# Four pieces of x in a row, early value weights and beta on another queue, keys ahead of queries: the start of a two-block attention kernel

## The chip, the cores and the metric

The kernel runs on one core of a Trainium2 chip. The metric is device time in microseconds (us) of one launch, as a median of several runs. The trace is one profiled execution, and all its times are counted from the start of its span. Engines are named TensorE (PE in the profile; PEld is its weight load), VectorE (DVE), ScalarE (ACT), GpSimd (POOL) and SyncE (SP, which only issues DMAs here).

## The reference, cut to what matters

Two attention blocks on separate inputs; the outputs are laid side by side. S is 2048, D is 1024, 32 heads of 32.

```
A:  q, k, v = x @ wqkv                       # heads of 32
    p = softmax(q k^T / sqrt(32));  out = (p v) @ wo
B:  q, k, v = x @ wq, x @ wk, x @ wv;  4 segments of 512 rows
    per segment: a_dot = softmax(q k^T / sqrt(32) + causal mask) v
                 a_mem = phi(q) M / (phi(q) z + 1e-6);  phi(t) = t + 1 if t > 0 else exp(t)
                 o = g a_mem + (1 - g) a_dot,  g = sigmoid(beta) per head
                 M += phi(k)^T v;  z += sum phi(k)
    out = o @ wo
```

## The kernel before, in words

Heads are handled four at a time (a group, 128 columns of the projections), eight groups in each block. Block A's scores are made in tiles of 128 keys x 256 queries per head. TensorE writes scores to PSUM (L1197), ScalarE turns two banks at a time into exponentials P (L1260 for the first eight, which take a bias; L1273 for the others), TensorE multiplies P with the values (L1364) and with ones for the row sums (L1371), VectorE and GpSimd normalize. For some A tiles a polynomial on VectorE and GpSimd (L1234, L1237) replaces one exponential. Projections (L825) run as jobs between the scores.

No maximum is taken per row. Instead a guard bounds the scores: squares of keys and queries (L1598 on GpSimd, L1836 on VectorE) are summed over a head's rows by a matmul (L1611), reduced to a column (L1618), made spreadable (`spreadable`, L1628: a copy to 32 columns times UP), spread over the partitions by another matmul (L1687) and reduced again (L1695). From that come a raw bias (L1701), a bias (L1704) and a flag (L1711). If the bound is small enough the exponential runs without a bias. ScalarE reads each guard's flag ahead of the first exponential that it covers and branches on it (`run_split`), so a late flag holds ScalarE. The first guard of A (of its first quarter of the rows) gives its raw bias directly to the first eight exponentials, without a branch. Later quarters of group 0 go through `guard_more`, which first takes the maximum with the running column (L1660).

The order of the work is not written out by hand. Every operation has a key (a place in the order of ScalarE's exponentials), a modelled duration and dependencies; `Prog.schedule` runs a list scheduler over all engines and so fixes one instruction order for each engine, which then executes in order. `deps` are waited for on the chip; `order` only says that an operation is not put ahead of another's start. `plan_jobs` adds the projections with release and due times. The table SHIFT moves keys of single items by hand-set amounts, one entry per item and engine.

The start (`plan_prologue`): `loads` issues group 0's key and query weights W_A on ScalarE's queue and six transposing loads of x on SyncE's (X_PIECES: quarter of the rows, range of the 128-column blocks, modelled issue and landing): pieces 0 and 1 are the first 512 rows, 2 and 3 the second 512, pieces 4 and 5 the third and the fourth whole. The first half of the value weights (Wv_A) is issued on SyncE between pieces 1 and 2. Piece 4 waits for piece 3 to land. TensorE runs idle warming products until piece 0 is there. `quarter(key, c, banks)` makes keys and queries of quarter c, in the order: keys, queries of blocks 0 to 3, then keys, queries of blocks 4 to 7. `job_V0` makes values: for each of four row blocks k eight products (L1881); its argument `behind` orders them behind another operation. `beta` (L1819 to L1828) loads beta and works out g; its item has key 60, so it runs during A's second group.

Of the kernel before, what the change touches and what calls it, by code (L numbers as in the profile page):

```python
# [7 lines left out]
ACT = mybir.ActivationFunctionType  # L8
# [3 lines left out]
P = 128  # L12
# [33 lines left out]
X_PIECES = ((0, 0, 4, 2.27, 5.3), (0, 4, 8, 4.81, 2.2), (1, 0, 4, 4.8, 2.1), (1, 4, 8, 1.82, 3.3), (2, 0, 8, 5.0, 3.0),  # L46
# [82 lines left out]
class Op:  # L129
# [4 lines left out]
    def __init__(self, eng, fn, dur, lat, key, mode=None, sem=None):  # L134
# [44 lines left out]
        1: -0.5}),  # L179
    ("plan_constants", "POOL", {  # L180
        0: -1.25, 3: 1.5, 4: -4.75, 5: -5.5, 6: 10, 8: -0.5, 9: -2.25, 10: -1.25, 15: 4, 16: -0.75, 17: 3.25, 19: 15.25,
        20: -3, 21: 12.25, 22: 1.5, 23: 5}),
    ("plan_exp", "POOL", {
# [8 lines left out]
    ("plan_jobs", "ACT", {  # L192
# [3 lines left out]
    ("plan_jobs", "DVE", {  # L196
# [65 lines left out]
    ("plan_prologue", "ACT", {  # L262
        4: 6, 5: 9.5, 8: -1.25, 10: -1.75}),
    ("plan_prologue", "DVE", {
        0: 2.5, 1: -5.5, 5: -0.25, 6: 0.25, 7: -0.25, 8: 4, 9: -0.5, 10: 1}),
    ("plan_prologue", "PE", {
# [2029 lines left out]
```

## Time and profile before

| | us |
|---|---|
| median of 3 runs (1050.74 to 1052.89) | 1052.52 |
| profiled execution | 1052.34 |
| its span | 1050.6 |
| ScalarE busy | 1016.4 |
| TensorE busy | 1020.6 |
| first products on x start | 7.36 |
| first exponential starts | 14.92 |
| ninth exponential starts | 24.88 |
| last exponential ends | 1041.9 |

A row of a timeline has its start, its length, engine, source line, operation, output<-input, shapes and count; in brackets stands the idle time of the engine before it and what ended it. Rows of one kind that follow one another are merged. A row of the DMA view ends with the us from issue to landing. A row of the table by stretches has the stretch, its length, each engine's busy time with its count of instructions, the granted clock, the share of the DMA engines and GB/s. TensorE's granted clock is 1.00 throughout.

### The profile page before, as it was taken

The numbers are of one execution on the slowest core, as the hardware profiler recorded it, in microseconds if no ns is written. First come the engines' busy times: TensorE is split into PE (matmuls) and PEld (weight loads), VectorE is DVE, ScalarE is ACT, GpSimd is POOL, SyncE is SP. The second block draws the span as 40 slices with busy tenths as digits, with TensorE's granted clock in tenths as the row PEclk, the third lists the DMA queues.
The fourth block names the chain that finished last, engine by engine and source line by source line (L and its number), as shares of the span: only waits on it lengthen the run. The fifth ranks groups of instructions, "written<-read, shape, count | busy, mean of one in ns | idle before, by whom it ended". The sixth has DMA issues, their size and how long they took to land.

```text
span 1050.6 us, 56208 instructions
## 1 busy us (share of the span) xinstructions
PE 1020.6 (97%) x25482; PEld 561.9 (53%) x25482; DVE 701.0 (67%) x1560; ACT 1016.4 (97%) x1225; POOL 585.7 (56%) x677
## 2 busy tenths in 40 slices
PE   8999999999999999999999999999999999999998
PEld 4555555655555545565555555565555545445554
DVE  2356767667566686787865598686765785874444
ACT  4999989999999999999999999999999999999997
POOL 2115577568554675766646487665644775663310
PEclk9999999999999999999999999999999999999999
DMA  9232442005313331033223320132113561021101
GB/s 184 40 91 59 78 119 45 20 6 126 89 43 90 66 100 29 11 83 66 63 62 95 96 62 19 27 92 54 51 28 86 162 177 30 24 78 61 51 23 63
DMA packets 171390, 72.17 MB, mean 69 GB/s; under 512 B 134800, under 2 KB 169360, under 8 KB 171152
## 3 DMA queue, kind: packets, MB, share of 16 engines
q1 hardware_dynamic: 168784, 67.79, 26.5%
q8 instruction: 200, 3.28, 1.3%
q10 hardware_dynamic: 2368, 0.79, 0.3%
q14 instruction: 38, 0.31, 0.1%
HBM read 45.29 MB, written 11.73 MB: 54 GB/s over the span
## 4 chain that ended last, share of the span: by engine, by line
PE 66%; ACT 30%; DVE 3%; issue 1%; ACTq 0%; DVEq 0%
PE ps L825 32%; ACT P L1273 28%; PE ps L1197 13%; PE ps L1364 9%; PE ps L1371 9%; PE ps L1881 1%; ACT P L1260 1%; ACT PKQ_B L1925 1%; DVE Y L1234 1%; DVE T L1434 1%; PE ps L1641 0%; DVE OT_B L1952 0%; DVE KQ_B L1584 0%; DVE T L1430 0%; DVE T L1436 0%
## 5 line engine op out<-in xcount | busy, mean ns | idle before, releaser
L1273 ACT ACTIVATE P<-ps 128x1024 bf16<-128x1024 f32 (+1 forms) x1176 | 988.6, 1062 | 13.7 <-DVE cu L1390 4.1
L1237 POOL TENSOR_TENSOR Pc<-Y 128x512 bf16<-128x512 f32 x238 | 249.5, 1049 | 259.9 <-PE ps L825 72.6
L1371 PE MATMUL ps<-P,onesb 128*32 128x256 bf16 (+1 forms) x4388 | 295.2, 270 | 0.2
L1364 PE MATMUL ps<-P,V_A 128*32 128x256 bf16 x3620 | 252.0, 274 | 0.3 <-ACT P L1273 0.2
L1234 DVE TENSOR_SCALAR Y<-ps 128x512 f32<-128x512 f32 x238 | 163.3, 686 | 104.7 <-PE ps L1197 97.8
L1197 PE MATMUL ps<-KQ_A 32*128 32x256 bf16 x4096 | 203.6, 273 | 12.5 <-ACT P L1273 7.2
L1197 PEld LDWEIGHTS ps<-KQ_A 32*128 32x128 bf16 x4096 | 61.9, 92 | 157.8 <-ACT P L1273 113.5
L1371 PEld LDWEIGHTS ps<-P,onesb 128*32 128x32 bf16 x4388 | 129.0, 96 | 26.3 <-issue 13.1
L825 PE MATMUL ps<-xT_B,W_B 128*32 128x512 bf16 (+1 forms) x2284 | 139.8, 359 | 1.2 <-DVE KQ_B L1584 0.4
L825 PE MATMUL ps<-xT_A,W_A 128*32 128x512 bf16 (+1 forms) x2256 | 138.3, 361 | 0.3 <-DVE V_A L1584 0.2
L1364 PEld LDWEIGHTS ps<-P,V_A 128*32 128x32 bf16 x3620 | 107.7, 96 | 26.0 <-issue 10.8
L1364 PE MATMUL ps<-Pc,V_A 128*32 128x256 bf16 x476 | 119.1, 274 | 1.1 <-issue 1.0
L1371 PE MATMUL ps<-Pc,onesb 128*32 128x256 bf16 x476 | 119.1, 274 | 0.7 <-issue 0.7
L1296 POOL TENSOR_SCALAR_AFFINE_SELECT P<-P 128x768 bf16<-128x768 bf16 (+1 forms) x96 | 75.7, 794 | 49.7 <-ACT P L1273 47.7
L1598 POOL TENSOR_TENSOR sqA<-KQ_A 128x512 bf16<-128x512 bf16 x61 | 63.3, 1047 | 62.7 <-DVE KQ_A L1584 29.3
L1598 POOL TENSOR_TENSOR sqB<-KQ_B 128x512 bf16<-128x512 bf16 x64 | 67.8, 1060 | 19.6 <-DVE KQ_B L1584 15.4
L825 PEld LDWEIGHTS ps<-xT_B,W_B 128*32 128x32 bf16 x2284 | 52.9, 96 | 47.1 <-issue 18.9
L825 PEld LDWEIGHTS ps<-xT_A,W_A 128*32 128x32 bf16 x2256 | 52.5, 96 | 46.5 <-issue 16.4
L1447 DVE STREAM_TRANSPOSE T<-rc 128x256 f32<-128x256 f32 (+1 forms) x152 | 72.6, 481 | 2.7
L825 PE MATMUL ps<-Wv_B,xT_B 128*32 128x512 bf16 (+1 forms) x1128 | 70.1, 361 | 1.1 <-issue 0.5
L825 PE MATMUL ps<-Wo_B,OT_B 128*32 128x512 bf16 (+1 forms) x1128 | 69.0, 361 | 0.2 <-DVE T L1430 0.2
L1584 DVE CAST KQ_B<-ps 128x512 bf16<-128x512 f32 x64 | 43.8, 684 | 35.0 <-PE ps L825 34.4
(117 smaller groups left out, 1229.2 us busy)
## 6 DMA issues: line engine op xcount, KB each, us to landing
Wv_B<-in_B_wv_dram SPq DMA_DIRECT2D x32, 256.0 KB, 3.4
W_B<-in_B_wk_dram SPq DMA_DIRECT2D x32, 256.0 KB, 3.3
W_B<-in_B_wq_dram SPq DMA_DIRECT2D x32, 256.0 KB, 4.0
Wo_B<-in_B_wo_dram SPq DMA_DIRECT2D x32, 256.0 KB, 3.1
out_dram<-outsb SPq DMA_DIRECT2D x56, 128.0 KB, 1.8
W_A<-in_A_wqkv_dram SPq DMA_DIRECT2D x14, 256.0 KB, 3.3
ot_a_scratch<-OTst SPq DMA_DIRECT2D x51, 64.0 KB, 1.8
xT_A<-ot_a_scratch SPq DMA_DIRECT2D x6, 512.0 KB, 5.4
```

Of the source, the lines that this page charges most:

```text
L825: ins = e.matmul(out[r], w[:, r], x, start=start, stop=stop, tile_position=(0, 32 * t), skip_group_check=True)
L1197: ins = e.matmul(out, kap, qap, start=st, stop=True, tile_position=(32 * h, 0), skip_group_check=True)
L1234: o = self.dve(lambda e: e.tensor_scalar(Y[:, :], src, KAPPA * SCALE, BETA, ALU.mult, ALU.add), 512, key - 9.0, [self.bank[bank]], [rY], f ...
L1237: last.append(self.pool(lambda e: e.tensor_tensor(dst, Y[:, :], Y[:, :], ALU.mult), 512, key - BCK, [rY], [rP], rate=0.56))
L1260: guarded = lambda e: e.activation(dst, src, ACT.Exp, bias=self.bias[:, bc:bc + 1], scale=SCALE)
L1273: a = self.act(guarded if early else lambda e: e.activation(dst, src, ACT.Exp, scale=SCALE), cols, key, rd, wr, fixed=EXP_FIXED + (0.095 i ...
L1296: self.pool(lambda e: e.affine_select(v, v, pattern=pat, compare_op=ALU.is_ge, fill=0.0, base=0, channel_multiplier=-1), 2 * nd * P, key + ...
L1364: ins = e.matmul(self.pb(obk, q0, q0 + nq, slice(32 * h, 32 * h + 32)), v, p, start=first, stop=last, tile_position=(0, 32 * h), skip_grou ...
L1371: ins = e.matmul(self.pb(obk, QC + q0, QC + q0 + nq, slice(32 * h, 32 * h + 32)), self.onesb[:, 0:32], p, start=False, stop=last, tile_pos ...
L1447: self.dve(lambda e: e.transpose(L2.rearrange("p (b r) -> p b r", r=32), bc), n, key, [rr], [rl], fixed=0.17)
L1584: self.dve(lambda e: e.tensor_copy(dst, src()), 512, key, [self.at(b)], rdst, fixed=0.155)
L1598: self.pool(lambda e: e.tensor_tensor(sq[:, :], src, src, ALU.mult), 512, key, [rsrc], [rs], rate=0.56)
```

## The change

- X pieces 0 to 3 are issued on SyncE one behind the other. Their modelled times change; piece 4 (and what had waited for piece 3 alone) now waits for pieces 2 and 3.
- The first half of the value weights is issued on ScalarE's queue, and waits there for piece 1 to land. Beta's load goes to ScalarE's queue behind W_A, its item gets key -98.9, and its margin goes.
- The second quarter's products run all keys first, then all queries, in a fixed order.
- The values of row block 1 are ordered behind the first guard's spread (`first_ge`) in place of its first matmul; those of row blocks 2 and 3 behind that spread in place of the first quarter's last product. Keys of these items move by about 50.
- In `guard_more` the maximum with the running column is taken inside the spreadable copy (one instruction instead of two); where a further guard follows, the maximum is still taken, off the chain. For the urgent guards the flag is worked out ahead of the bias.
- SHIFT gets new entries: 1907 before, 1926 after, 1803 of them new, gone or different.

```
-X_PIECES = (... (1, 0, 4, 4.8, 2.1), (1, 4, 8, 1.82, 3.3), ...
+X_PIECES = (... (1, 0, 4, 2.0, 2.2), (1, 4, 8, 2.0, 2.4), ...
...
-    def spreadable(self, key, src, rsrc, port=True, urgent=None):
+    def spreadable(self, key, src, rsrc, port=True, urgent=None, least=0.0):
-        ... tensor_scalar(dg, src().to_broadcast([P, 32]), UP, None, ALU.mult)
+        ... tensor_scalar(dg, src().to_broadcast([P, 32]), least, UP, ALU.max, ALU.mult)
...
     def guard_more(...)
-        o = self.dve(... tensor_tensor(cols[ci], cols[ci], cols[c0], ALU.max) ..., key + 0.1)
-        o.urgent = True
-        self.colrun = (ci, rc)
-        self.guard_end(key + 0.2, [self.colrun], 2, [new], bank=self.xr.grp, urgent=True)
+        dg = self.spreadable(key + 0.1, lambda: self.cols[:, ci:ci + 1], [rc, r0], urgent=True, least=self.cols[:, c0:c0 + 1])
+        if i is not None:
+            o = self.dve(... tensor_tensor(cols[ci], cols[ci], cols[c0], ALU.max) ..., key + 0.3)
+            self.colrun = (ci, rc)
+        self.guard_end(key + 0.2, [dg], 2, [new], bank=self.xr.grp, urgent=True)
...
     def guard_end(...)
+            if urgent:
+                nf, o = flagged()          # the flag, as before behind the bias
             self.last_bias = ...
...
     def loads(key):
                 if n == 3:
-                    gate = o
+                    gate = {last, o}
...
                 if n == 1:
-                    self.load_WAv(0, key, 0, 1)
+                    self.load_WAv(0, key, 0, 1, 2.8, "ACT").deps.add(o)
...
     def quarter(key, c, banks):
-            for i, kq in [(i, kq) for lo in (0, 4) for kq in range(2) for i in range(lo, lo + 4)]:
+            for i, kq in [(i, kq) for kq in range(2) for i in range(8)] if c else [... as before]:
+                    if was:
+                        o.order.add(was)
+                    was = o
...
-        self.item(-49.0, lambda key: self.job_V0(0, 0, key, 5, self.last_gc, self.last_bias, hi=2))
-        self.item(-47.5, lambda key: self.job_V0(0, 0, key, 7, self.last_quarter, lo=2))
-        self.item(-48.0, lambda key: quarter(key, 1, (6, 7)))
-        self.item(-47.0, lambda key: self.job_V0(0, 1, key, None, self.last_ge))
+        self.item(-49.0, lambda key: self.job_V0(0, 0, key + 50.5, 5, self.last_gc, self.last_bias, hi=2))
+        self.item(-47.5, lambda key: self.job_V0(0, 0, key + 52.0, 7, self.first_ge, lo=2))
+        self.item(-48.0, lambda key: quarter(key + 48.0, 1, (6, 7)))
+        self.item(-47.0, lambda key: self.job_V0(0, 1, key + 53.0, None, self.last_ge))
...
     def beta(key):
-            self.dma(lambda e: e.dma_start(self.graw[:, :], src), self.sm_beta, key, [], [r], lat=4.0, gate=True)
+            self.dma(lambda e: e.dma_start(self.graw[:, :], src), self.sm_beta, key, [], [r], lat=4.5, eng="ACT").order.add(self.r_WA[0][1].w[-1])
-                x.margin = 20.0 if k == 0 else 0.0
-        self.item(60.0, beta)
+        self.item(-98.9, beta)
...
     def job_V0(...)
-                    o.order.add(behind)
+                    o.order.add(behind if k != 1 else self.first_ge)
```

More of the change, by code (lines that the diff above doesn't have):

```diff
@@ L1545, in load_xB, with turn @@
         self.turn(self.xTB[:, :, :], xb[L * s:L * s + L, :], self.sm_xTB, key, [], [self.r_xTB], 5.0, 3.4, True)
-    def turn(self, dst, src, sem, key, reads, writes, issue, lat, gate=False):
+    def turn(self, dst, src, sem, key, reads, writes, issue, lat, gate=False, eng="SP"):
         return self.dma(lambda e: e.dma_start(dst, src, transpose=True), sem, key, reads, writes,
-                        issue=issue, lat=lat, gate=gate)
+                        issue=issue, lat=lat, gate=gate, eng=eng)
     def xbank(self):
@@ L1659, in guard_more @@
         c0, r0 = self.colrun
[L1660 to L1664 removed]
+        dg = self.spreadable(key + 0.1, lambda: self.cols[:, ci:ci + 1], [rc, r0], urgent=True, least=self.cols[:, c0:c0 + 1])
+        if i is not None:
+            o = self.dve(lambda e: e.tensor_tensor(self.cols[:, ci:ci + 1], self.cols[:, ci:ci + 1], self.cols[:, c0:c0 + 1], ALU.max), 1,
+                         key + 0.3, [rc, r0], [rc])
+            self.colrun = (ci, rc)
+        self.guard_end(key + 0.2, [dg], 2, [new], bank=self.xr.grp, urgent=True)
         if i is None:
@@ L1703, in guard_end, with flagged @@
                                                              ALU.add, ALU.mult), 1, key + 0.4, [rr], [rraw], fixed=0.2)
-            self.last_bias = self.pg.ops[-1] if raw_bias else self.dve(lambda e, bc=bc, raw=raw: e.tensor_scalar(
+            braw = self.pg.ops[-1]
+            def flagged():
+                nf = self.nflag
+                self.nflag += 1
+                o = self.dve(lambda e, nf=nf, raw=raw: e.tensor_scalar(
+                    self.flags[:, nf + 1:nf + 2], raw, -FREE, self.flags[:, nf:nf + 1], ALU.is_ge, ALU.min), 1,
+                    key + 0.4, [rraw, self.r_flags], [self.r_flags], fixed=0.2)
+                return nf, o
+            if urgent:
+                nf, o = flagged()
+            self.last_bias = braw if raw_bias else self.dve(lambda e, bc=bc, raw=raw: e.tensor_scalar(
                 self.bias[:, bc:bc + 1], raw, -FREE, raw, ALU.is_lt, ALU.mult), 1, key + 0.4, [self.r_braw], [rb], fixed=0.2)
@@ L1708, in guard_end @@
                          key + 0.4, [rb], [self.r_biasr[bc]])
-            nf = self.nflag
-            self.nflag += 1
-            o = self.dve(lambda e, nf=nf, raw=raw: e.tensor_scalar(
-                self.flags[:, nf + 1:nf + 2], raw, -FREE, self.flags[:, nf:nf + 1], ALU.is_ge, ALU.min), 1,
-                key + 0.4, [rraw, self.r_flags], [self.r_flags], fixed=0.2)
+            if not urgent:
+                nf, o = flagged()
             self.flag_of[bc] = (nf, o, self.flags[0:1, nf + 1:nf + 2].bitcast(dt.int32))
@@ L1761, in loads @@
                 if n == 1:
-                    self.load_WAv(0, key, 0, 1)
+                    self.load_WAv(0, key, 0, 1, 2.8, "ACT").deps.add(o)
                 if n == 4:
                     for kq in range(2):
-                        self.load_WA(1, kq, key).deps.add(gate)
-            self.load_WAv(0, key, 1, 2).deps.add(gate)
+                        self.load_WA(1, kq, key).deps.update(gate)
+            self.load_WAv(0, key, 1, 2).deps.update(gate)
         self.item(-99.0, loads)
         def quarter(key, c, banks):
-            for i, kq in [(i, kq) for lo in (0, 4) for kq in range(2) for i in range(lo, lo + 4)]:
+            was = None
+            for i, kq in [(i, kq) for kq in range(2) for i in range(8)] if c else [(i, kq) for lo in (0, 4) for kq in range(2) for i in range(lo, lo + 4)]:
                     b = banks[kq]
```

26 lines of the change are left out of this document (12 added, 14 removed), and 359 rows, old and new, of the table SHIFT.

## The prediction, made before the changed kernel was run

> **What bounds the kernel now.** I read the page's first part, then the table by stretches (each has its length, then each engine's busy time), then TensorE's waits and ScalarE's timeline.
>
> ```profile
> span 1050.6 us, 56208 instructions
> PE 1020.6 (97%) x25482; PEld 561.9 (53%) x25482; DVE 701.0 (67%) x1560; ACT 1016.4 (97%) x1225; POOL 585.7 (56%) x677
> ```
> ```profile
> 14.92:24.88 9.96, 8.26 (x167) 4.62 (x160) 5.03 (x14) 8.15 (x8) 1.04 (x1) 1.00 0.91 185
> 24.88:147.00 122.12, 118.74 (x2825) 68.50 (x2826) 74.77 (x162) 117.31 (x144) 47.99 (x48) 1.00 0.34 74
> 147.00:1041.90 894.90, 874.73 (x22206) 479.80 (x22198) 614.29 (x1369) 887.16 (x1068) 530.75 (x592) 1.00 0.25 64
> ```
> ```profile
> PE ps L1197 <- ACT P L1273: 9.6, 23, 1.1
> ```
> ```profile
> 14.92 8.15 ACT L1260 ACTIVATE P<-ps,bias 128x1024 bf16<-128x1024 f32 x8 [2.79 <-DVE bias L1701]
> 24.88 1.94 ACT L1273 ACTIVATE P<-ps 128x1024 bf16<-128x1024 f32 x2 [1.81 <-PE ps L1881]
> ```
>
> ScalarE and TensorE are both busy for 97%, so I ask which waits. From 147.00 to 1041.90 ScalarE idles 894.90 - 887.16 = 7.74 us; TensorE idles 894.90 - 874.73 = 20.17, much of it on ScalarE (the 9.6 us row, over the whole run). ScalarE's row of exponentials is therefore the tighter bound: a microsecond counts if it makes that row start sooner or takes a hole out of it. The exponentials themselves are not touched. The holes: the start (first exponential at 14.92), 1.81 before 24.88, 122.12 - 117.31 = 4.81 up to 147.00, and the 7.74.
>
> The profiled execution took 1052.34 us, 1.74 more than its span; the median is 1052.52. I sum from 1052.34 and let 1.74 stand.
>
> **The change part by part.** *x and the early value weights.* SyncE's issues (start, length), and below them single issues with the us from issue to landing: W_A's first and piece 0 (piece 1 has the same 6.4), then the value weights and piece 2, then piece 3:
>
> ```profile
> 2.29 4.41 SPq L1549 DMA_TRANSPOSE xT_A<-in_A_x_dram  x1
> 6.75 0.57 SPq L1526 DMA_DIRECT2D Wv_A<-in_A_wqkv_dram  x1
> 7.38 4.40 SPq L1549 DMA_TRANSPOSE xT_A<-in_A_x_dram  x1
> ```
> ```profile
> 11.81 1.99 SPq L1549 DMA_TRANSPOSE xT_A<-in_A_x_dram  x1
> ```
> ```profile
> W_A<-in_A_wqkv_dram ACTq DMA_DIRECT2D x1, 256.0 KB, 3.3
> xT_A<-in_A_x_dram SPq DMA_TRANSPOSE x1, 6.4
> ...
> Wv_A<-in_A_wqkv_dram SPq DMA_DIRECT2D x1, 256.0 KB, 5.4
> xT_A<-in_A_x_dram SPq DMA_TRANSPOSE x1, 6.6
> ...
> xT_A<-in_A_x_dram SPq DMA_TRANSPOSE x1, 4.5
> ```
> ```profile
> 10.20:11.70 1.50, 1.50 (x35) 0.83 (x31) 0.83 (x2) 0.65 (x2) 0.00 (x0) 1.00 0.30 18
> 11.70:13.70 2.00, 2.00 (x41) 0.96 (x34) 0.89 (x3) 0.43 (x1) 0.00 (x0) 1.00 1.02 229
> ```
>
> Piece 1 lands at 2.29 + 6.4 = 8.7, the weights at 6.75 + 5.4 = 12.15, piece 2 at 7.38 + 6.6 = 14.0, piece 3 at 11.81 + 4.5 = 16.3. Between 10.20 and 11.70 only 18 GB/s moved, against 229 just after: the third transpose, behind a plain load, sat with the engines free. Issued at 6.75, straight behind another transpose, piece 2's issue costs between 1.99 (piece 3 behind piece 2) and 4.41 (piece 1 behind piece 0, where W_A's 512 KB moved too). I take 1.99, because that pair has no cold start in it: piece 3 issues at about 8.8 and would land at 13.3; the value weights' 256 KB beside it cost half a microsecond, so 13.8, with 15.7 as the other end.
>
> ```profile
> 11.05 0.60 ACT L1792 ACTIVATE sqA<-ps 128x512 bf16<-128x512 f32 x1 [8.28 <-PE ps L825]
> ```
>
> The weights now stand on ScalarE's queue and wait for piece 1 (8.7). Behind them on ScalarE are only beta's exponential and the evictions of the first quarter, from 11.05 on; the 8.28 us of waiting before them hide the issue. From issue to landing I have 3.3 (same size, same queue, little beside it) to 5.4 (this load, behind a transpose). I take 4.0, for they share with piece 2: landing at 12.75. Piece 4 waits for pieces 2 and 3 and so moves forward with piece 3; all that SyncE has behind it follows.
>
> The Trainium skill, page "DMA: Bandwidth & Descriptors", section "Issuing engines are not separate DMA queues", says that transfers from SyncE's and ScalarE's queues interleave on the same 16 DMA engines, so that a second issuer saves only issue time. The idle 1.50 us in the row above speak against its being all here. Its result is a rival below.
>
> *First exponential.* TensorE, then VectorE:
>
> ```profile
> 12.79 0.40 PE L1881 MATMUL ps<-Wv_A,xT_A 128*128 128x128 bf16 x4
> 13.12 0.40 PE L1197 MATMUL ps<-KQ_A 32*128 32x256 bf16 x8
> 13.44 0.84 PE L1881 MATMUL ps<-Wv_A,xT_A 128*128 128x128 bf16 x12
> 14.22 0.19 PE L1687 MATMUL ps<-pick,dg 128*32 128x16 bf16 x4
> ```
> ```profile
> 12.93 0.18 DVE L1628 TENSOR_SCALAR dg<-cols 128x32 bf16<-128x32 f32 x1
> ```
>
> The guard's spread (L1687) has its input at 12.93 + 0.18 = 13.11 but stands behind 16 value products. The change lets eight of them start only with the spread. Eight times (14.22 - 13.44) / 12 = 0.065 is 0.52: spread at 13.70, first exponential at 14.40. At best it goes at 13.11, 1.11 sooner. If the weights land after 12.79 every microsecond of that is lost again, since TensorE runs in order. I take 0.45 sooner: 14.47, and eight exponentials end at 14.47 + 8.15 = 22.62.
>
> *The ninth exponential* (24.88) needs the second guard's flag. TensorE's last products of the second quarter, then VectorE's steps:
>
> ```profile
> 18.43 0.83 PE L825 MATMUL ps<-xT_A,W_A 128*32 128x512 bf16 x12
> ```
> ```profile
> 19.10 1.29 DVE L1787 CAST KQ_A<-ps 128x512 bf16<-128x512 f32 x2 [3.63 <-PE ps L825]
> ...
> 22.34 0.16 DVE L1660 TENSOR_TENSOR cols<-cols 128x1 f32<-128x1 f32 x1
> ...
> 23.86 0.21 DVE L1704 TENSOR_SCALAR bias<-braw 128x1 f32<-128x1 f32 x1
> 23.99 0.20 DVE L1711 TENSOR_SCALAR flags<-braw,flags 128x1 f32<-128x1 f32 x1
> ```
>
> Products end at 19.26, the ninth exponential starts 5.62 later. Keys first: of the two casts (1.29) one is done while the queries' products run, saving 0.60. The one-element maximum leaves the chain: 0.16. The flag ahead of the bias: 23.99 - 23.86 = 0.13. Left: 4.73. The products began behind the spread (14.22 + 0.04) and took 5.00, of which 0.9 was waiting for piece 3 and for ScalarE. With piece 3 at 13.8 I give them 4.3 from 13.86: 18.2, and 18.2 + 4.73 = 22.9, just behind 22.62. The ninth starts **2.0 us** earlier. Bounds: at best the exponentials run through (14.92 - 1.11 + 8.15 = 21.96: 2.9 earlier); at worst, with the weights at 8.75 + 6.6 = 15.35 (the slowest of the landing rows), the spread is 2.1 late, the ninth follows at about 25.1, 0.3 later than now. The maximum that remains for the next guard is one 0.16 us step off the chain, while VectorE waits for the spread anyway.
>
> *Beta.*
>
> ```profile
> 106.85 0.21 ACT L1826 ACTIVATE gc<-gc 128x8 f32<-128x8 f32 x1 [0.64 <-DVE gc L1823]
> 106.97 1.49 ACT L1273 ACTIVATE P<-ps 128x1024 bf16<-128x1024 f32 x2
> ```
>
> ScalarE loses 106.97 - 106.21 = **0.76** here. After the change load, casts and exponential fall into the same 8.28 us. If that cover failed (beta landing after 11) the first quarter's casts would wait behind beta's on VectorE; but the load is issued behind W_A's two (0.8 + 3 x 0.57, the weights' issue, is 2.5), and even 6.6 later is 9.1.
>
> *The planner's table.* 1803 entries of SHIFT differ, so the order of jobs changes everywhere. One hole stands out:
>
> ```profile
> 146.86 3.77 ACT L1273 ACTIVATE P<-ps 128x1024 bf16<-128x1024 f32 x4 [4.10 <-DVE cu L1390]
> ```
> ```profile
> 145.45 0.69 DVE L1430 TENSOR_TENSOR T<-ps,cu 128x512 f32<-128x512 f32 x1 [1.01 <-PE ps L1371]
> 146.06 0.20 DVE L1704 TENSOR_SCALAR bias<-braw 128x1 f32<-128x1 f32 x1
> 146.18 0.20 DVE L1711 TENSOR_SCALAR flags<-braw,flags 128x1 f32<-128x1 f32 x1
> ```
>
> The brackets name the releaser by time; what came last is the flag at 146.18 of B's first pair of head groups, held behind a normalization (145.45) that waited for TensorE. In the table this guard's job (plan_jobs 154) goes from 3.75 to -1.5 on TensorE, and the query product before it (153) loses its 2.25 on GpSimd, so the guard should come sooner; but ScalarE arrives 2.8 sooner too. The wait lies between nothing (4.1 gained) and 4.10 + 2.76 (the lead of 2.0 + 0.76 lost). I take half of 4.1: **2.0** gained. The other 7.74 are drawn anew, from none to twice as much; I take no change.
>
> Sum: 1052.34 - 2.0 - 0.76 - 2.0 = **1047.6 us**.
>
> **The rivals.**
> *The wait before 146.86 goes entirely*: 1052.34 - 2.0 - 0.76 - 4.1 = 1045.5. For it: the guard moves forward in the table. Against: its product does not (153 stays near 19 on TensorE).
> *TensorE takes the lead back by 147.* It idles only 9.96 - 8.26 = 1.70 from 14.92 to 24.88 and 3.38 after that up to 147.00. If only the 1.70 can be won, 1050.6. Against: many of its jobs there can be put off.
> *One issuer more frees nothing*: piece 2 comes sooner only by 7.38 - 6.75 = 0.63, piece 3 lands at 15.7, products end at about 19.0, the ninth exponential starts at 23.7, 1.2 sooner: 1048.4. This is what the Trainium skill's rule, above, would give.
> *The weights land late on ScalarE's queue* (5.4 as before: 14.15): spread at 15.1, ninth at 24.1, 0.8 sooner: 1048.8. Then the change does not do what it says for the first exponential, which would be later than 14.92.
> *Slower: a second late flag.* Each guard's flag is read by ScalarE in order, and the new table may put another one behind a normalization as at 146.18. If the first eats the lead and one more costs 4.1: 1052.34 + 4.1 = 1056.4. It decides from the point where ScalarE's idle time between the ninth exponential and the last exceeds 4.81 + 7.74 + 2.0 + 2.1 = 16.7.
>
> **How the numbers follow.** Chances: forecast 0.40 (1046 to 1049.5 by itself), wait gone 0.20, one issuer more 0.10, late weights 0.06, lead taken back 0.13, second late flag 0.11. This kernel can be told from no change at about 0.2%, 2.1 us: faster is below 1050.4, slower above 1054.6. Faster 0.40 + 0.20 + 0.10 + 0.06 = 0.76; same 0.13; slower 0.11. The range reaches down to 1042.6 (2.9 at the start, 0.76, 4.1 and 2.0 of the 7.74) and up over the lead taken back, to 1052.5.
>
> **What would show it.** Right: pieces 2 and 3 with issues of about 2 us and piece 3 landed before 14.5; the spread ahead of 14; first exponential near 14.5 and ninth near 22.9 with less than 0.5 idle before it; no beta wait near 106; before B's first exponentials a wait of about 2. Wrong: a 4.4 us issue for piece 2, value products waiting for Wv_A after 12.8, or a new wait of over 2 us for a flag later on.

## The result, and the profile after

The changed kernel takes 1054.16 us (median of 11 runs, 1053.16 to 1057.64) against 1050.8 for the kernel before (11 runs, 1049.72 to 1052.89): the ratio is 1.0032, with a 95% interval from 1.0022 to 1.0041. It is slower, where faster by 0.5% was forecast, and lies above the range's upper end of 1052.5. The profiled execution took 1054.58, with a span of 1052.8.

First the page's head, then ScalarE's timeline of the start (start, length, engine, line, operation, output<-input, shapes, count; in brackets the idle time before it and what ended it):

```profile
span 1052.8 us, 56133 instructions
PE 1020.9 (97%) x25442; PEld 562.4 (53%) x25442; DVE 701.7 (67%) x1559; ACT 1016.3 (97%) x1225; POOL 586.7 (56%) x677
```
```profile
7.13 0.39 ACTq L1832 DMA_DIRECT2D graw<-in_B_beta_dram  x1
12.64 0.21 ACT L1838 ACTIVATE gc<-gc 128x8 f32<-128x8 f32 x1 [9.87 <-DVE gc L1836]
12.64 0.37 ACTq L1527 DMA_DIRECT2D Wv_A<-in_A_wqkv_dram  x1
...
17.48 2.12 ACT L1261 ACTIVATE P<-ps,bias 128x1024 bf16<-128x1024 f32 x2 [3.33 <-DVE bias L1703]
21.10 2.12 ACT L1261 ACTIVATE P<-ps,bias 128x1024 bf16<-128x1024 f32 x2 [1.51 <-PE ps L1198]
23.97 4.13 ACT L1261 ACTIVATE P<-ps,bias 128x1024 bf16<-128x1024 f32 x4 [0.75 <-PE ps L1198]
29.08 3.77 ACT L1274 ACTIVATE P<-ps 128x1024 bf16<-128x1024 f32 x4 [0.98 <-PE ps L1372]
```

The busy totals are those of before within 1.0 us for every engine; what moved is the start. Beta's load is issued at 7.13, not near 2.5, and the exponential of beta, which stands ahead of the value weights' load in ScalarE's queue, holds that load until 12.64. The first exponential starts at 17.48 (before: 14.92), the first eight are torn apart twice, and the ninth starts at 29.08 (before: 24.88). VectorE and TensorE in the same stretch:

```profile
11.85 0.75 DVE L1836 CAST gc<-graw 32x8 f32<-32x8 bf16 x4 [10.62 <-DMA graw<-in_B_beta_dram]
...
13.41 0.68 DVE L1800 CAST KQ_A<-ps 128x512 bf16<-128x512 f32 x1
```
```profile
10.61 1.25 PE L826 MATMUL ps<-sqB 128*32 128x512 bf16 x20
14.65 0.29 PE L1612 MATMUL ps<-sqA,blk 128*32 128x256 bf16 x4 [2.79 <-ACT KQ_A L1806]
...
16.00 0.29 PE L1893 MATMUL ps<-Wv_A,xT_A 128*128 128x128 bf16 x1 [0.41 <-DMA Wv_A<-in_A_wqkv_dram]
```

VectorE's first work is beta's casts; they wait for beta's landing until 11.85, and the first quarter's cast, which was ready near 10.8, follows at 13.41. TensorE has nothing to do for 2.79 us. Then comes something that the trace of before never showed. The table by stretches (stretch, its length, each engine's busy time, the granted clock, DMA share, GB/s), first of the one window before the clock's change, then of the start and the rest:

```profile
12.21:15.62 3.41, 0.94 (x16) 0.38 (x16) 2.49 (x9) 1.29 (x3) 0.00 (x0) 1.00 1.07 234
```
```profile
15.00:18.00 3.00, 2.59 (x36) 1.55 (x29) 1.19 (x5) 0.53 (x1) 0.00 (x0) 0.60 0.73 162
18.00:22.00 4.00, 4.00 (x43) 1.45 (x44) 0.42 (x1) 2.49 (x3) 0.00 (x0) 0.50 1.13 255
22.00:25.00 3.00, 2.90 (x52) 0.92 (x40) 0.74 (x2) 2.25 (x4) 1.04 (x1) 0.93 0.64 131
25.00:29.08 4.08, 3.49 (x75) 2.31 (x76) 2.87 (x11) 3.10 (x4) 0.00 (x0) 1.00 1.22 255
29.08:147.00 117.92, 116.55 (x2748) 67.17 (x2746) 70.92 (x146) 116.91 (x142) 45.78 (x46) 1.00 0.28 62
147.00:1045.00 898.00, 876.19 (x22274) 482.29 (x22262) 619.74 (x1378) 887.06 (x1068) 533.99 (x595) 1.00 0.26 65
```

TensorE is granted half its clock from 15.6 to 22.4 (0.60, 0.50, 0.93), behind a window in which it worked 0.94 of 3.41 us. This is no feature of the one profiled execution: the mean granted clock of all eleven runs is 0.994 to 0.998, where 93 of the 107 runs of the kernel before that were taken beside the experiments have 1.000. The eight first exponentials with their scores then take 29.08 - 17.48 = 11.60 us, where before they took 24.88 - 14.92 = 9.96. From the ninth exponential to the end of the last it is 1045.0 - 29.1 = 1015.9 against 1041.9 - 24.9 = 1017.0, and the tail behind it 7.8 against 8.7: 2.0 us gained there, 4.2 lost at the start, together the 2.2 by which the spans differ.

Nor is the middle as smooth as it could be. TensorE's largest waits that no other engine ends ("issue"), and ScalarE's holes behind them:

```profile
151.44 0.61 PE L826 MATMUL ps<-xT_B,W_B 128*32 128x512 bf16 x6 [1.72 <-issue]
...
464.74 1.60 PE L826 MATMUL ps<-Wv_A,xT_A 128*32 128x256 bf16 x50 [1.07 <-issue]
...
696.34 0.29 PE L1198 MATMUL ps<-KQ_B 32*128 32x256 bf16 x3 [1.43 <-issue]
```
```profile
149.11 1.94 ACT L1274 ACTIVATE P<-ps 128x1024 bf16<-128x1024 f32 x2 [2.91 <-PE ps L826]
152.44 1.02 ACT L1274 ACTIVATE P<-ps 128x1024 bf16<-128x1024 f32 x1 [1.39 <-PE ps L1198]
...
466.72 1.94 ACT L1274 ACTIVATE P<-ps 128x1024 bf16<-128x1024 f32 x2 [1.15 <-PE ps L1198]
...
696.67 1.94 ACT L1274 ACTIVATE P<-ps 128x1024 bf16<-128x1024 f32 x2 [1.28 <-PE ps L1198]
```

The first of these stalls stands inside a row of 40 projection products of one line, and no engine's step ends where it ends. So there are three suspects: beta's late load (with the value weights behind it), the halved clock, and these stalls (1.39 + 1.15 + 1.28 = 3.8 us of ScalarE). The runs below tell them apart. Beta's own mechanism was read in the code: where an operation is ordered behind another of the same engine and close to it, emission turns the order into a wait, and the semaphore of a load counts up when it has landed. The times agree: W_A's second half landed at 7.11, and beta's load went out at 7.13.

```
                o.deps |= {x for x in o.order if x.eng == e and n - x.pos <= 12 and not (o.prog and x.prog)}
```

The section ahead of the prediction said that an order only keeps an operation from being put ahead of another's start. That holds for the planner, not for this line.

### The profile page after: what moved, and what is told of

The parts are those of the page before. It is cut to its first block, busy times and chain, and to the rows that moved or that the text cites. A ratio compares the mean times of both kernels' runs of the same rounds, so it can differ in the third digit from the quotient of the medians.

```text
span 1052.8 us, 56133 instructions
## 1 busy us (share of the span) xinstructions
PE 1020.9 (97%) x25442; PEld 562.4 (53%) x25442; DVE 701.7 (67%) x1559; ACT 1016.3 (97%) x1225; POOL 586.7 (56%) x677
## 4 chain that ended last, share of the span: by engine, by line
PE 65%; ACT 28%; DVE 3%; issue 2%; DMA 1%; POOL 1%; ACTq 0%; DVEq 0%
PE ps L826 32%; ACT P L1274 27%; PE ps L1198 13%; PE ps L1365 9%; PE ps L1372 9%; PE ps L1893 1%; ACT PKQ_B L1937 1%; DMA W_A<-in_A_wqkv_dram 1%; PE ps L1642 0%; DMA graw<-in_B_beta_dram 0%; DVE T L1435 0%; DVE Y L1235 0%; DMA Wv_A<-in_A_wqkv_dram 0%; POOL P L1297 0%; DVE OT_B L1964 0%
## 5 line engine op out<-in xcount | busy, mean ns | idle before, releaser
L1599 POOL TENSOR_TENSOR sqA<-KQ_A 128x512 bf16<-128x512 bf16 x61 | 62.8, 1039 | 65.6 <-DVE KQ_A L1585 29.1
```

Source lines behind the costliest of these rows:

```text
L1599: self.pool(lambda e: e.tensor_tensor(sq[:, :], src, src, ALU.mult), 512, key, [rsrc], [rs], rate=0.56)
```

## The experiments

Every kernel below was timed against the kernel before on the same chip; the ratios are to it. The order of instructions on each engine stays that of the kernel that an experiment starts from, unless a move is told. The kernel before took 1050.70 to 1050.93 (medians) beside all of them, so their times can also be set against each other, and against the changed kernel's 1054.16.

**e1: beta's load without the wait.**

```
-  {x for x in o.order if x.eng == e and n - x.pos <= 12 ...}
+  {x for x in o.order if x.eng == e and x.sem is None and n - x.pos <= 12 ...}
```

> The changed kernel with every instruction in the same place on its engine; only beta's load no longer waits on ScalarE for the landing of W_A's second piece (7.1 us). Theory 1, beta's wait: the load is issued at about 1.9, beta's casts and exponential are done before the first quarter's products, the value weights are issued near 8.8 and land by 13.2, the first exponential starts at 14.4 to 14.9 in place of 17.48, the ninth near 22.9 in place of 29.08, TensorE's clock stays at 1.00, and the time falls by about 6 us against the changed kernel: 2 to 3 us under the kernel before. Rival A, the new order of the table costs the time: the start gets better, but the kernel stays above the kernel before. Rival B, the value weights are late on ScalarE's queue whatever beta does: they land after 14 and the first exponential stays behind 15.5.

Measured: 1052.26 (1049.95 to 1054.36), ratio 1.0010 [1.0000, 1.0019]. ScalarE's timeline, then TensorE's:

```profile
1.90 1.06 ACTq L1832 DMA_DIRECT2D graw<-in_B_beta_dram  x1
...
9.30 0.38 ACTq L1527 DMA_DIRECT2D Wv_A<-in_A_wqkv_dram  x1
...
15.53 8.15 ACT L1261 ACTIVATE P<-ps,bias 128x1024 bf16<-128x1024 f32 x8 [3.16 <-PE ps L1893]
24.66 4.69 ACT L1274 ACTIVATE P<-ps 128x1024 bf16<-128x1024 f32 x5 [0.98 <-PE ps L1372]
...
36.16 1.94 ACT L1274 ACTIVATE P<-ps 128x1024 bf16<-128x1024 f32 x2 [2.06 <-PE ps L1198]
```
```profile
33.83 1.73 PE L826 MATMUL ps<-xT_A,W_A 128*32 128x512 bf16 x28 [2.04 <-DMA xT_A<-in_A_x_dram]
```

The start is repaired by 4.4 us: the first exponential comes 1.95 sooner and the eight take 9.13 in place of 11.60, since the clock no longer falls there. But the value weights, issued at 9.30, still hold the first exponential beyond 14.92, and x's last piece comes late (2.04 us of TensorE, 2.9 of ScalarE). The stall near 150 (1.45) is there again, another of 2.10 stands near 467, and none near 695. Some 6 us were expected against the changed kernel, 1.9 came. Beta's wait is a cause, and not the only one; rival B, late value weights whatever beta does, held (landing at 14.29, first exponential at 15.53).

**e2: TensorE kept busy.** The changed kernel, with the first five of the warming products behind the first quarter issued four times.

```
-            for _ in range(n):
-                o = self.pe(lambda e: self.mm4(e, ...
+            for k in range(n):
+                o = self.pe(lambda e, t=4 if behind and k < 5 else 1: [self.mm4(e, ...) for _ in range(t)][-1], ...
```

> The changed kernel, beta's wait kept, with the five warming products behind the first quarter made four times as long, so that TensorE is busy from 10.4 to about 14.7, where it now idles for 2.79 us. It adds work that nothing uses. If the lower granted clock (0.50 from 18 to 22 us) comes from that idle time, the clock stays at 1.00, the first exponential stays near 17.3, the ninth comes 2 to 3 us sooner than 29.08, and the time falls by 2 to 3 us: about half of the loss at the start is the clock, the rest the wait itself. If the clock has nothing to do with the idle time, the ninth exponential and the time stay as they are within 0.5 us.

Measured: 1048.8 (1048.02 to 1049.77), ratio 0.9980 [0.9971, 0.9989]: 5.4 us faster than the changed kernel, and faster than the kernel before with the new order of the planner's table untouched, so that order as such is not what costs the time. The first exponential is where it was, the clock stays whole, the eight run through:

```profile
17.47 8.14 ACT L1261 ACTIVATE P<-ps,bias 128x1024 bf16<-128x1024 f32 x8 [3.05 <-PE ps L1893]
26.59 1.02 ACT L1274 ACTIVATE P<-ps 128x1024 bf16<-128x1024 f32 x1 [0.98 <-PE ps L1372]
```

That gives 29.08 - 26.59 = 2.5 us. The other 3 came from the middle, where all three stalls were gone, and the run itself could not say why: it changes the clock and the number of products at once.

**e3: beta alone, in the kernel before.** Beta's load, casts and exponential moved by hand to the places and the wait that they have in the changed kernel; all else as before.

> The kernel before, in its own order, with beta alone moved by hand as the change has it: load on ScalarE behind W_A with the wait for its second piece to land, casts ahead of the first quarter's cast on VectorE, exponential ahead of the first quarter's evictions on ScalarE. Everything else, the value weights on SyncE too, as before. Theory 1: beta lands near 11.9, the first exponential starts near 17.3 in place of 14.92, the clock falls, the ninth exponential starts at 27 to 29 in place of 24.88, 0.76 us come back near 106, and the kernel is 2 to 3.5 us slower than before. Rival B (the value weights' new queue is what costs): no more than 0.5 us slower, since they keep their old queue.

Measured: 1052.25 (1048.71 to 1054.2), ratio 1.0014 [1.0003, 1.0025]. VectorE, then ScalarE:

```profile
11.10 0.76 DVE L1823 CAST gc<-graw 32x8 f32<-32x8 bf16 x4 [9.87 <-DMA graw<-in_B_beta_dram]
```
```profile
16.48 8.15 ACT L1260 ACTIVATE P<-ps,bias 128x1024 bf16<-128x1024 f32 x8 [3.41 <-DVE bias L1701]
26.44 1.02 ACT L1273 ACTIVATE P<-ps 128x1024 bf16<-128x1024 f32 x1 [1.81 <-PE ps L1881]
```

Beta's move alone costs 1.56 us at the start (14.92 to 16.48) against the 0.76 it saves near 107, and makes the kernel slower by 1.5 us in the medians. That is less than the 2 to 3.5 expected: TensorE idled only 1.22 us before the guard's sums, and the clock did not fall (1.00).

**e4: e1 and e2 together.**

> The changed kernel with beta's load free of the wait for W_A (as in e1) and with longer warming (as in e2). Theory (the loss is two things that add up: beta's wait and the half clock after TensorE's idle window): the clock at the start stays 1.00, the ninth exponential comes near 24.7 as in e1, 1.9 sooner than in e2, so about 1048.8 - 1.9 = 1046.9. Rival (beta's 8 KB load beside the transposes slows x's pieces): the third quarter of x lands late again, TensorE waits about 2 us for it near 31.8 as in e1, and the time is 1048.8 to 1050.

Measured: 1048.55 (1047.57 to 1050.05), ratio 0.9980 [0.9971, 0.9989]. The two do not add up: the longer warming runs until 15.2 and itself holds the first exponential at 17.23 (ninth 26.37). The theory's 1046.9 missed because I had not counted the warming's own 4.3 us on TensorE.

**e5: the longer warming in the kernel before.**

> The kernel before with the same longer warming. Theory (the warming repairs only what the change broke): no difference to the kernel before within 0.1%, first exponential 14.9, ninth 24.9. Rival (warming is worth something by itself, since executions of the kernel before hide clock drops at the start that its one profile doesn't show): 1 to 2 us faster.

Measured: 1055.79 (1054.07 to 1056.87), ratio 1.0042 [1.0028, 1.0056]. Both expectations fell. The warming runs until 15.4, the first exponential moves to 18.17 and the ninth to 28.12; a stall of 1.41 near 469 comes on top. So warming is worth nothing by itself; it filled a hole in e2 that beta's wait had made.

**e6 and e7: beta back, and the value weights back as well.** Both with e2's longer warming. In e6, beta's load goes to SyncE near 78 and its casts and exponential to 103; e7 adds the value weights' load on SyncE between pieces 1 and 2.

> The changed kernel with longer warming, and beta's load, casts and exponential put back to SyncE near 78 us and VectorE and ScalarE near 103 us; all else in the changed kernel's order. Theory (only beta held the first guard): the first cast of keys is back near 10.8, the value weights' load is issued at about 8.8 and lands by 12.1 to 12.8, first exponential 14.5, ninth 23 to 23.5, with 0.76 us lost again near 103: about 1048.8 - 3.3 + 0.8 = 1046.3. Rival (the value weights land late on ScalarE's queue whatever beta does, 5 us and more after their issue, as in e1): they land near 14, first exponential 15.3 to 15.5, ninth 24.5: 1047.5 to 1048.

> As e6, and the first half of the value weights issued on SyncE between pieces 1 and 2, as in the kernel before. Theory (moving the value weights is worth something): pieces 2 and 3 land 1.2 and 1.5 later than in e6, the ninth exponential 0.5 to 1 later. Rival (late weights are the cost of the move): the weights land near 12.2 to 12.9, first exponential 0.5 to 1 sooner than in e6, ninth no later: 0 to 1 us faster than e6.

Measured: 1051.57 (1050.5 to 1053.19), ratio 1.0011 [1.0002, 1.0020], and 1051.88 (1050.18 to 1052.97), ratio 1.0011 [1.0002, 1.0021]. Neither could answer: the warming again sets the first exponential (17.43 and 17.19), and beta's new place brought a wait of its own (1.98 us at 112.72 in e6; 1.3 us of beta's casts stand on VectorE at 106.53, ahead of the polynomial that TensorE then waits for).

**e8: sixty more products, no more work.** The 15 x 4 warming products ahead of x, each split in two of 256 columns, in the changed kernel.

```
-  [mm4(e, ps[:, 512 * 5:512 * 6], dummy[:, 0:P], dummy[:, :], True, True)]
+  [mm4(e, ps[:, 512 * 5 + c:512 * 5 + c + 256], dummy[:, 0:P], dummy[:, c:c + 256], True, True) for c in (0, 256)]
```

> The changed kernel with each of the 15 x 4 warming products ahead of x split in two of 256 columns: 60 more TensorE instructions, the same work, nothing else moved. In e2 and e4, which have 60 products more than the changed kernel, three stalls of TensorE without a releaser (1.72 near 149.7, 1.07 near 463.7, 1.43 near 694.9) are gone. Theory (these stalls hang on where a product falls in TensorE's stream of instructions, which is fetched in blocks of 16 KB, and not on the clock or on beta): the start stays as in the changed kernel (half clock from 15 us on, ninth exponential near 29), the three stalls go, and the time is 1054.2 - 3.8 = 1050.4. Rival (the stalls follow from the late start): they stay, no difference to the changed kernel, 1054.

Measured: 1049.7 (1047.71 to 1051.56), ratio 0.9989 [0.9980, 0.9998]: 4.5 us faster than the changed kernel, for a split that does no work. The stalls near 150, 464 and 695 are gone. But the clock did not fall either, because piece 1 landed at 10.15 in place of 8.78, so that the warming behind the first quarter ran later, into the hole that beta leaves. Again both at once. The profiled execution is also the fastest of e8's eleven; five of the others have a mean granted clock of 0.997 or 0.998, so in some of them the clock did fall.

**e9, e10: the split with beta free, and x's last piece sooner.** e9 is e1 with the split of e8; e10 also issues x's last piece on SyncE ahead of the second group's W_A and the second half of the value weights.

> e1 (beta's load without the wait for W_A) with the same 60 more products ahead of x, and no longer warming. Theory (three things: beta's wait, the clock, the fetch stalls): first exponential near 15.5 and ninth near 24.7 as in e1, the rest as in e2 and e4 (span less ninth 1020.3), so 1045.0 of span and 1046.8 us, or 2.9 more (1049.7) if the fourth quarter of x comes late again. Rival (layout does nothing): 1052.3 as e1.

> As e9, and x's last piece issued on SyncE ahead of the second group's W_A and the second half of the value weights, which it had behind it in none of the others. Theory (in e1 TensorE waited 2.04 us for that piece and ScalarE then 2.9, and the clock fell for a window): piece 5 lands about 2.3 sooner, the wait near 31.8 goes, 1046.8 at most. Rival (the transposes, not their place in the queue, set when piece 5 lands): no difference to e9.

Measured: 1048.25 (1046.68 to 1049.96), ratio 0.9972 [0.9962, 0.9982], and 1047.04 (1045.3 to 1048.34, 5 runs), ratio 0.9964 [0.9951, 0.9978]. e10 has the lowest median here, 3.8 us below the kernel before, though its interval overlaps those of e9 and e13. Its table by stretches behind the ninth exponential, from its fastest execution (1045.3):

```profile
25.44:147.00 121.56, 120.00 (x2825) 68.71 (x2826) 73.19 (x157) 118.73 (x145) 49.51 (x49) 1.00 0.30 72
147.00:1038.40 891.40, 874.44 (x22250) 481.44 (x22246) 619.35 (x1372) 884.76 (x1067) 530.63 (x592) 1.00 0.25 65
```

The start is still no better than before (ninth at 25.44; 24.88 before); the gain is behind it. The last piece lands at 28.5 in place of 32.4 in e9, and no wait for it is left. e9 had none either in its profile, so this move's worth is not shown.

**e11: the split in the kernel before.**

> The kernel before with the same 60 more products ahead of x. Theory (fetch stalls hang on the place in the stream): its stalls near 144, 609 and 657 (0.96, 1.12, 0.99) move or change, as in e5, where new ones stood near 107 and 469; the start stays (14.9 and 24.9); between 1049 and 1053. Rival: nothing changes, 1050.8.

Measured: 1053.18 (1050.83 to 1054.99), ratio 1.0020 [1.0011, 1.0029]. The stalls moved: 1.64 near 466 and 1.39 near 848 are new, and piece 1 landed 1.4 late. The one near 144 is gone; the idle times near 609 and 657, which the expectation counted in, are not of this kind (ScalarE and VectorE end them) and are still there. What helps the one kernel by 4.5 us hurts the other by 2.4, of which 1.1 is the later ninth exponential (26.01) behind piece 1.

**e12: clock and stalls told apart.** The changed kernel with the split behind the first quarter (five times four products of 512 columns into 16 of 128), so that TensorE's hole stays.

> The changed kernel with the first 5 x 4 warming products behind the first quarter split in four of 128 columns: 60 more TensorE instructions as in e8, but behind the first quarter, so that the first 16 KB fetch of instructions stays near 9 and doesn't meet piece 1 (in e8 to e11 the fetch came at 8.1 and piece 1 landed at 10.2 in place of 8.7 to 9.3). TensorE's idle time before 14.65 stays, so this tells the half clock from the fetch stalls, which e2 and e8 changed together. Theory (two separate losses): the clock falls as in the changed kernel, ninth exponential near 29, but the stalls near 150, 464 and 695 are gone: 1054.2 - 3.8 = 1050.4. Rival (the stalls come from the half clock): they are there again, 1054.

Measured: 1050.8 (1048.82 to 1052.63), ratio 0.9999 [0.9990, 1.0008]. Table by stretches and ScalarE's timeline:

```profile
10.85:14.18 3.33, 1.25 (x84) 1.07 (x76) 1.50 (x8) 0.94 (x3) 0.00 (x0) 1.00 0.91 188
14.18:21.01 6.83, 5.97 (x60) 2.86 (x60) 2.35 (x8) 2.48 (x3) 0.00 (x0) 0.50 1.11 197
```
```profile
28.82 1.02 ACT L1274 ACTIVATE P<-ps 128x1024 bf16<-128x1024 f32 x1 [0.99 <-PE ps L1372]
...
148.85 4.69 ACT L1274 ACTIVATE P<-ps 128x1024 bf16<-128x1024 f32 x5 [2.91 <-PE ps L826]
```

As the theory had it: the clock falls for 6.83 us, the ninth exponential stays late (28.82), and the hole of 1.39 behind 149 is gone, as are the other two. The stalls are worth 1054.16 - 1050.8 = 3.4 us (3.8 by the holes) and do not come from the clock. e12 and e2 have the same number of products and differ by the hole and the half clock behind it: 2.2 us in the ninth exponential, 2.0 in the medians. Within e12, the ten runs with a mean clock of 0.995 to 0.998 take 1049.63 to 1052.63, the one with 1.000 takes 1048.82.

**e13, e14: the value weights.** e13 is e10 with e12's split in place of e8's; e14 also has the value weights on SyncE again.

> As e10 (beta free, x's last piece sooner), with the 60 more products as in e12 in place of those ahead of x. Theory: piece 1 lands near 9.2 as in e1, first exponential 15.5 and ninth 24.7, the rest 1018.2 of span as in e10: 1042.9 of span, median 1046. Rival (piece 1's lateness of 1 us in e10 is hidden behind the late value weights): first exponential 16.3, no difference to e10.

> As e13, and the first half of the value weights back on SyncE between pieces 1 and 2, without its wait for piece 1 to land. Tells what moving this load cost, which the longer warming hid in e6 and e7. Theory (the move costs, since the load goes out only when piece 1 has landed and then shares with pieces 2 and 3): the weights land at 12.3 as in e7 and the kernel before, first exponential 14.3 to 14.5, about 1 us sooner than in e13; pieces 2 and 3 land near 14.1 and 16.4, so the second guard is later and a wait of about 1 us stands before the ninth exponential: within 0.5 us of e13. Rival (the move gains what was wanted, x sooner): ninth exponential 0.5 to 1.5 later than in e13 and as much slower.

Measured: 1048.12 (1046.39 to 1049.6), ratio 0.9971 [0.9960, 0.9981], and 1049.13 (1046.48 to 1050.59), ratio 0.9984 [0.9974, 0.9993]. ScalarE in e13, then in e14, and TensorE in e14:

```profile
15.76 2.12 ACT L1261 ACTIVATE P<-ps,bias 128x1024 bf16<-128x1024 f32 x2 [3.77 <-PE ps L1893]
19.05 6.29 ACT L1261 ACTIVATE P<-ps,bias 128x1024 bf16<-128x1024 f32 x6 [1.17 <-PE ps L1198]
26.32 1.94 ACT L1274 ACTIVATE P<-ps 128x1024 bf16<-128x1024 f32 x2 [0.98 <-PE ps L1893]
```
```profile
14.09 4.13 ACT L1261 ACTIVATE P<-ps,bias 128x1024 bf16<-128x1024 f32 x4 [2.12 <-PE ps L1893]
21.42 4.13 ACT L1261 ACTIVATE P<-ps,bias 128x1024 bf16<-128x1024 f32 x4 [3.20 <-PE ps L1198]
26.86 1.94 ACT L1274 ACTIVATE P<-ps 128x1024 bf16<-128x1024 f32 x2 [1.31 <-PE ps L1372]
```
```profile
17.86 2.53 PE L826 MATMUL ps<-xT_A,W_A 128*32 128x512 bf16 x28 [2.07 <-DMA xT_A<-in_A_x_dram]
```

With the weights back on SyncE the first exponential comes 1.67 sooner and x's piece 3 later (17.82 in place of 15.73), for which TensorE waits 2.07. Moving the weights trades the first exponential for the ninth: 0.5 sooner in the trace, about 1.0 us in the medians, whose intervals overlap. In both, TensorE's wait for a load (1.64 for the weights in e13, 2.07 for x in e14) was followed by a window at half clock, so the runs do not settle which place is better. Within e13, the three runs with a mean clock of 1.000 take 1046.39 to 1047.46, the five below it 1047.89 to 1049.6. So e13's first exponential came as expected (15.76), but the ninth 1.6 later than the 24.7 expected, and e13 is no faster than e10.

## Why the prediction was wrong, point by point

The span came out 7.0 us longer than forecast (1052.8 against 1047.6 - 1.74). Of that, 6.2 lie before the ninth exponential (29.08 against 22.9): beta's wait 1.95, the half clock 2.5, the late value weights 1.1 and the second guard 0.7, each worked out below. The other 0.8 lie behind it.

*Beta.* This is the step that failed: "the load is issued behind W_A's two (0.8 + 3 x 0.57, the weights' issue, is 2.5), and even 6.6 later is 9.1". It was issued at 7.13 and landed at 11.83. I took the order behind W_A for a place in the queue; it was a wait for W_A's landing. The text even named what follows if beta lands after 11 (the first quarter's casts wait behind beta's), but gave it no price. Its price: 1.95 us of first exponential (17.48 to 15.53, e1), 1.56 in the kernel before (e3); the 0.76 near 107 was saved as forecast.

*The clock.* No term at all. The granted clock is 1.00 throughout in the profile of before, and I asked of no step what TensorE would do while it waited. Beta's wait emptied a window, and the half clock cost 11.60 - 9.13 = 2.5 us (e1, e2). The two make up the 4.4 us by which the start differs between the changed kernel and e1.

*The value weights.* In the changed kernel the 4.0 us from issue to landing was not the trouble (it took 3.3); the issue was: it stood behind beta's exponential and went out at 12.64, landing at 15.95. Without beta's wait (e1) the issue came at 9.30 in place of 8.75, since piece 1 landed at 9.28, and the landing took 5.0. "Behind them on ScalarE are only beta's exponential and the evictions" had the order of the queue the wrong way round. The forecast for the first exponential, 14.47, was reached only with the weights back on SyncE (14.09, e14). That is the rival of late weights, and even without beta's wait it held (landing at 14.29 in e1; first exponential at 15.53, 1.1 behind the forecast).

*x in a row.* The issues were forecast well for piece 2 (2.13 us, forecast 1.99) and for the start of piece 3 (8.76, forecast 8.8). The mis-sized term is piece 3's time from issue to landing, 5.0 in the sum. The issue and its time to landing, in the changed kernel and then in e1:

```profile
8.76 3.76 SPq L1550 DMA_TRANSPOSE xT_A<-in_A_x_dram  x1
```
```profile
xT_A<-in_A_x_dram SPq DMA_TRANSPOSE x1, 6.1
```
```profile
9.25 4.66 SPq L1550 DMA_TRANSPOSE xT_A<-in_A_x_dram  x1
```
```profile
xT_A<-in_A_x_dram SPq DMA_TRANSPOSE x1, 6.7
```

Piece 3 landed at 14.82 in the changed kernel (16.32 before; forecast 13.8), but there the value weights went out only at 12.64. Where they go out near 9, as the change meant it, piece 3 lands at 15.94 (e1), 16.26 (e4), 15.78 (e6) and 15.73 (e13); where they go out near 13, at 15.02 (e2) and 15.10 (e12). The rival of one issuer more gave 15.7, so with the change as it was meant these landings agree with the rival, and not with the forecast. The sooner x was of no use behind a later first guard.

*The ninth exponential.* Forecast 22.9, with less than 0.5 idle; in every version with the new order 0.98 to 1.31 us stand before it, and the best was 24.66 (e1), 0.2 sooner than before. The new order of the second guard did bring something: from the first exponential to the ninth it is 9.12 to 9.14 us in all eight versions whose eight exponentials run through (e1, e2, e4, e6 to e10), where the kernel before has 9.96. The sum had 22.9 - 14.47 = 8.43, 0.7 too little. From the end of the second quarter's products the ninth takes 4.18 in the changed kernel and 4.20 in e14, less than the 4.73 of the sum. But the second guard still comes last: its flag ends 0.68 to 0.70 before the ninth exponential starts, in the kernel before and in all versions with the new order. Its steps on TensorE stand behind scores that wait for exponentials, so it moves with the exponentials; no run moved it by itself. With beta and the clock repaired, the 2.0 us were therefore not there: the first exponential was late by the weights, and the ninth followed it at 9.13.

*The middle.* Forecast 2.76 gained (0.76 and 2.0); measured 1.1 from the ninth exponential to the last, and 0.9 in the tail, which the forecast had left alone. Without the three stalls the middle gains 4.3 (e2: 1012.7 against 1017.0 before, worked out as above) or 3.6 (e12: 1013.4). The wait before 146.86 went from 4.10 to 2.91, of which a stall at once gave back 1.39. That the planner's table did even this is not shown. TensorE has a stall of the same kind just before that wait in the kernel before, and in e11, where sixty more products took it away, the wait is 2.69 with the old table. TensorE in the kernel before, then ScalarE in e11:

```profile
145.00 0.28 PE L1364 MATMUL ps<-Pc,V_A 128*32 128x256 bf16 x1 [0.96 <-issue]
```
```profile
146.43 3.77 ACT L1273 ACTIVATE P<-ps 128x1024 bf16<-128x1024 f32 x4 [2.69 <-PE ps L825]
```

So the prediction gave to the table what was at least in part the place of the stream.

*The slower rival*, a second late flag, did not happen: ScalarE's idle time from the ninth exponential on is 1.01 + 10.94 = 11.95 us, below the 16.7 from which it was to decide. The time did come out slower, but for a reason that I had not named. That e10 and e13 come out near the forecast is no confirmation of it: they get there with a start that gains nothing and a middle that gains more (1010.3 in e10's fastest execution against 1017.0); how much of that is the new order and how much the absence of stalls, no run tells.

What is settled: beta's wait (e1, e3), the half clock (e2, which fills the hole, and e12, which keeps it) and the stalls (e12) cost about 1.6 to 2, 2 to 2.5 and 3.4 us. What stays open is why a stall sits at one place of the stream and not at another.

## What to carry to other kernels

Before costing a moved load by its issue, look at how its order is emitted: a dependency on another load is a wait for its landing, and everything behind it on that queue, and behind its consumers on theirs, inherits it. Where a step may leave TensorE idle at the start, price the half clock that follows as a term of its own. And two versions of a kernel that differ by a few microseconds may differ only in where TensorE's stream of instructions falls: shift the stream by some products that cost nothing before believing in the difference.

## What the runs showed of the hardware that was not expected

*The clock.* The granted clock falls in whole windows of 3.41 us. Worked out from the gaps between products, in the profiles of the changed kernel and the experiments (e9's has no clock record): there are 12 falls between the start-up and the last exponential, in eight profiles, and each followed a window in which TensorE was idle for 1.42 to 2.47 us in all; no window with less than 1.42 was followed by one, and four with 1.43 to 1.72 were not either. The Trainium skill, page "TensorE: Matmul & The Clock Gate", section "Part 1: The HAM clock gate (the "warmup" mystery)", has the free-running window of that length and the half rate after an idle window; the traces agree on the length (3.41, or 6.83 for two windows) and on the half rate, but 1.42 us of idle time, less than half a window, could already be enough.

*TensorE's stream of instructions.* The changed kernel's page has this row among its DMA queues:

```profile
q8 instruction: 200, 3.28, 1.4%
```

200 packets of 16 KB for 25442 products and as many weight loads, about 64 bytes each: the stream is fetched while the program runs, a block for every 128 products or so. They start 5.2 us apart on average. One of them started at 149.27, took 0.93 us, and the stall of 1.72 began at 149.72. The other stalls bear this out. From 30 to 1041 us, the profiles of all sixteen kernels together have 25 waits of TensorE of over 0.4 us that no engine and no load ends. Each began 0.42 to 2.44 us behind the start of such a packet, but every one ended 2.17 to 2.90 us behind it. Of the 175 waits of that size that an engine or a load ends, 26 do. So what ends a stall goes with the fetch; no run moved a fetch alone.

The stalls also hang on the place in the stream. The one near 150 sat at the same product in the changed kernel and in e1 (the 3139th), the one near 467 at the same product in e5 and e11 (the 11384th). In the new order, the changed kernel and e1 have stalls of 1.07 to 2.10, and none of the ten versions with 60 more products has one above 0.96. Place is not all: the second stall of the changed kernel stands behind 11126 products, that of e1 behind 11253, and the third has none to match it in e1.

*A fetch beside the transposes.* With 60 products more ahead of x, the first packet came at 8.1 to 8.3, in the middle of piece 1, in place of 8.9 to 10.9. In all four such kernels (e8 to e11) piece 1 landed at 10.13 to 10.28; in the other profiles, at 8.66 to 9.28. The two went together four times of four; that the fetch held piece 1 back is not shown by itself.
